# Values by groups of heads, map sums on GpSimd, an earlier first block of rows and 125 VectorE steps in a gated mix of two attentions

## The chip, the cores and the metric

One core of one Trainium2 chip runs the kernel. The metric is the device time of one execution in microseconds, as the median of several runs. The profile is of one further execution.

## The reference, cut to what matters

The input x has 2048 rows of 512 channels; there are 32 heads of 16 channels. Two attentions are computed from x and mixed row by row.

```
g = sigmoid((x * gate_w).sum(-1))
A: q, k, v = x @ A_wqkv, by heads;  pq = q @ w_phi[h];  pk = k @ w_phi[h]
   phi = concat(softmax(p), softmax(-p))          # 32 values per head and row
   kv = phi_k^T v;  z = sum of phi_k over rows
   o = (phi_q kv) / (phi_q z + 1e-6);  a = o @ A_wo
B: q, k, v = x @ B_wqkv, by heads
   o = softmax(q k^T / 4) v;  b = o @ B_wo
out = g * a + (1 - g) * b
```

The softmax of B over 2048 x 2048 scores for each of 32 heads is nearly all of the work: 134 million exponentials.

## The kernel before, in words

**Sets and steps.** B is computed in 32 sets: four blocks of 512 query rows (`qc`), in each four groups of 8 heads (`g`), in each the even and the odd heads (`par`). A set has 16 steps, one for each tile of 128 keys. A step makes the scores of 4 heads in two halves of 128 keys x 1024 (two heads with 512 queries each) on TensorE (L752, `qk`), takes the exponential of both halves, and multiplies with the values on TensorE into one PSUM bank `O` of the set (L794 and L807, `pv`).

**Two ways to take an exponential.** Most steps use ScalarE: two ACTIVATE instructions of 128 x 1024 (L771). NDVE gives for each set the number of steps that VectorE takes instead: two conversions of scores to 16-bit integers (L761, `di`), then over both halves a mask (L777, `dm`), a product (L780, `dw`) and a second mask (L784, `de`). Such a step has two value products. NDVE sums to 117, and its first two entries are 1 and 1. In a set the VectorE steps take the first key tiles, and ScalarE the others in order.

**Values and keys.** `k_proj` (L488) projects 512 rows of keys for one group of heads; its evacuation is on ScalarE for group 0 (L494) and on VectorE for the others (L497). `v_proj` (L525) makes the values of all 32 heads for two tiles of 128 rows at once: 8 matmuls of 512 columns and one VectorE evacuation of 128 x 1024 (L532, seen at the helper's line L469). All sixteen tiles are made in sets 1 and 2. Queries come from `q_proj` (L500). For the first set they are evacuated and multiplied with four masks from SBUF (L510); for the others eight small transfers on SyncE's queue spread the heads (L521).

**Attention A** runs in the gaps. `phi` (L625), 16 times for the keys and 16 times for the queries, makes a map of 128 rows: four matmuls, two exponentials of 128 x 512 on ScalarE (L634), a sum over 16 columns of each of 64 groups on VectorE (L636, TENSOR_REDUCE), an addition on GpSimd for the final check (L638), a reciprocal on VectorE (L640) and a product on GpSimd (L641). Four exponent buffers lie in WAT's memory. Key maps start at unit 100 and follow every 16 units, query maps at 400 and every 32; a set has 32 units, of time as the planner has it.

**The start.** x0 (512 rows, L405) is loaded on SyncE's queue and transposed on TensorE through PSUM (L550), copied by ScalarE and VectorE in halves (L553, L554). Three DMA transposes (L409) bring the other 1536 rows, one after the other, into xT. ScalarE's queue issues five weight loads of B (L412 to L416): group 0 of keys and queries, all values, the other keys, the other queries. Then SyncE issues the DMA transpose of A's weights (WAT, L417), A's values, and the gate.

**Order.** All instructions are given to a planner (`_Sched`) with a priority and a cost. It simulates the five engines and fixes the order on each engine; at run time each engine is strictly in order and waits on semaphores. GpSimd's instructions and VectorE's `dm`, `dw`, `de` and `qm` are `shared`: in the plan the one waits for the other. `est` delays TensorE's use of VectorE's and GpSimd's results by SLACK (0.6). PSUM: a ring `R` of three score tiles used by ScalarE's and VectorE's steps alike, one bank `O`, one bank `M` for all else. Eight buffers `E` hold exponentials; the first 24 exponentials go to memory of phiK and vA instead.

Of the kernel before, what the change touches and what calls it, by code (L numbers as in the profile page):

```python
# [6 lines left out]
BF16 = mybir.dt.bfloat16  # L7
# [6 lines left out]
D = 512  # L14
H = 32
# [18 lines left out]
VROW = H * VW + 16  # L34
NDVE = [1, 1, 4, 4, 4, 3, 4, 4, 3, 4, 3, 4, 4, 3, 5, 4, 4, 3, 4, 3, 5, 3, 4, 4, 5, 3, 4, 4, 4, 3, 5, 4]
LEAD = 3.0
# [10 lines left out]
STAY = 1.0  # L47
PAIRS = (0, 1, 2, 3, 4, 5, 6, 7)
RUSH = 1.5
HOLD = 0.4  # L50
WARM = 10
RUSH_K = 20.0
RUSH_O = 25.0
RUSH_1 = 8.0
QLEAD1 = 28
LATE_A = 0
VLEAD = 3.0
KLEAD1 = 24
KLEAD = 40
QLEAD = 32  # L60
EARLY = 8.0
T0 = 12.0
# [267 lines left out]
def _build(ctx, nc, A_x, A_wqkv, A_w_phi, A_wo, B_wqkv, B_wo, gate_w, out):  # L330
# [19 lines left out]
    vB_ = sb([128, NT, VROW], name="vB")  # L350
    vB = vB_[:, :, 0:H * VW].rearrange("p t (h c) -> p t h c", c=VW)
    vA = sb([128, NT, 8, 66], name="vA")
# [22 lines left out]
    eA_r = _Slots([watv[:, 1024 * i:1024 * (i + 1)] for i in range(4)])  # L375
# [28 lines left out]
    xs = D_all[0].bitcast(BF16).rearrange("p (i c) -> p i c", c=D)  # L404
    op_x0 = dma("sp", -100, 3.6, xs, A_x[0, 0:NQ, :].rearrange("(i p) c -> p i c", p=128), name="x0")  # L405
    op_x = [None]
    for c in range(1, QC):
        op_x.append([add("sp", -100 + c, 2.5,
                         lambda e, c=c: e.dma_start_transpose(xT[:, :, NQ * c:NQ * (c + 1)], A_x[0, NQ * c:NQ * (c + 1), :]),  # L409
                         name=f"x{c}", dma=7.0)])  # L410
    wbv = B_wqkv.rearrange("(t p) c -> p t c", p=128)
    op_wk0 = dma("act", -100, 4.0, W_Bk[:, :, 0:128], wbv[:, :, D:D + 128], name="wk0")  # L412
    op_wq0 = dma("act", -99, 4.0, W_Bq[:, :, 0:128], wbv[:, :, 0:128], name="wq0")
    op_wv = dma("act", -98, 6.0, W_Bv[:], wbv[:, :, 2 * D:3 * D], name="wv")
    op_wk1 = dma("act", -97, 8.0, W_Bk[:, :, 128:D], wbv[:, :, D + 128:2 * D], name="wk")
    op_wq1 = dma("act", -96, 8.0, W_Bq[:, :, 128:D], wbv[:, :, 128:D], name="wq")  # L416
    op_wat = add("sp", -90, 3.0, lambda e: e.dma_start_transpose(WAT[:], A_wqkv[:, 0:2 * D]), name="wat", dma=3.0)  # L417
# [7 lines left out]

    t0, t1, t2, t3 = (mtmp[:, i, :] for i in range(4))
# [13 lines left out]
    op_vpad = [pool(-99, 0.2, lambda e: e.memset(vB_[:, :, H * VW:VROW], 0.0), name="vpad")]  # L440
# [30 lines left out]
    def fill(prio, tile, off, lhs, rhs, deps, name, rush=0.0):  # L471

        f = None
        for t in range(KT):
            f = add("pe", prio - rush + 0.01 * t, MM, lambda e, t=t: e.matmul(  # L475
                tile.ap[:, off:off + 512], lhsT=lhs(t), rhs=rhs(t), start=(t == 0), stop=(t == KT - 1)),
                deps=list(deps) + [f], tiles=[tile], mode="full", name=name, nb=max(0.0, prio - EARLY))
            fills.append(f)
        return f
# [8 lines left out]
    def k_proj(g, c, prio, tile, off, eng="dve"):  # L488
        f = fill(prio, tile, off, lambda t: W_Bk[:, t, 128 * g:128 * (g + 1)],
                 lambda t: xT[:, t, NQ * c:NQ * (c + 1)], op_x[c] + [op_wk1 if g else op_wk0], f"kf{g}{c}", RUSH_K if g != 1 else RUSH_1)  # L490
        use_wk.append(f)
        dst, src = (lambda: kT[:, g, NQ * c:NQ * (c + 1)]), (lambda: tile.ap[:, off:off + 512])
        if eng == "act":
            ev_k[g, c] = add("act", prio, 0.478, lambda e: e.activation(dst(), src(), ACTF.Copy, scale=KFAC),  # L494
                             deps=[f], tiles=[tile], name=f"kev{g}{c}")
        else:
            ev_k[g, c] = add("dve", prio - RUSH_K, 0.6, lambda e: e.tensor_single_scalar(dst(), src(), KFAC, ALU.mult),  # L497
                             deps=[f], tiles=[tile], name=f"kev{g}{c}")

    def q_proj(g, c, prio, tile, off):  # L500

        f = fill(prio, tile, off, lambda t: W_Bq[:, t, 128 * g:128 * (g + 1)],
                 lambda t: xT[:, t, NQ * c:NQ * (c + 1)], op_x[c] + [op_wq1 if g else op_wq0], f"qf{g}{c}", RUSH_K if (g, c) != (1, 0) else RUSH_1)
        qt = q_t[g, c] = _Tile(q_r)
        if (g, c) == (0, 0):
            q3 = lambda: qt.ap[:, 3, :]
            ev = evac("dve", prio, q3, lambda: tile.ap[:, off:off + 512], [f], [tile, qt], name=f"qev{g}{c}")
            ms = []
            for j in range(4):
                ms.append(add("dve", prio + 0.01 * j, 0.39, lambda e, j=j: e.tensor_scalar(  # L510
                    qt.ap[:, j, :], q3(), masks[:, j:j + 1], None, op0=ALU.mult),
                    deps=[ev, op_masks] + (ms if j == 3 else []), tiles=[qt], name=f"qm{g}{c}{j}"))
            ev_q[g, c] = ms
            for o in op_qz:
                o.deps.extend(ms)
            return
# [8 lines left out]
    def v_proj(st, n, prio):  # L525

        tile = _Tile(M_r if n == 1 else R_r)
        fs = [fill(prio, tile, 512 * i, lambda t, i=i: xT[:, t, 128 * (st + i):128 * (st + i + 1)], lambda t: W_Bv[:, t, :],
                   op_x[st // 4] + [op_wv], f"vf{st}") for i in range(n)]
        use_wv.extend(fs)  # L530
        src = lambda: tile.ap[:, 0:512 * n].rearrange("p (t h d) -> p t h d", t=n, d=16)
        e1 = evac("dve", prio, lambda: vB[:, st:st + n, :, 0:16], src, fs, [tile], n=512 * n, name=f"vev{st}")  # L532
        for i in range(n):
            ev_v[st + i] = e1
# [7 lines left out]
    tx = _Tile(R_r)  # L542
    txv = lambda: tx.ap.bitcast(BF16).rearrange("p (t q) -> p t q", q=NQ)
    xtp = []
    for t in range(KT):

        def fn(e, t=t):
            ins = None
            for i in range(4):
                ins = e.transpose(txv()[:, t, 128 * i:128 * (i + 1)], xs[:, i, 128 * t:128 * (t + 1)], ident[:])  # L550
            return ins
        xtp.append(add("pe", -80 + t, 0.3, fn, deps=[op_x0, op_id], tiles=[tx], mode="full", name="xtp"))
    op_x[0] = [add("act", -80, 0.9, lambda e: e.copy(xT[:, 0:2, 0:NQ], txv()[:, 0:2, :]), deps=xtp[0:2], tiles=[tx], name="xev"),  # L553
               add("dve", -80, 0.6, lambda e: e.tensor_copy(xT[:, 2:4, 0:NQ], txv()[:, 2:4, :]), deps=xtp[2:4], tiles=[tx], name="xev")]  # L554
    I_r.tenant[0] = _Tile(None)
    I_r.tenant[0].ops = xtp
    tq = _Tile(R_r)
    k_proj(0, 0, -50, tq, 0, "act")
    q_proj(0, 0, -49, tq, 512)
    tk1 = _Tile(R_r)  # L560
    k_proj(0, 1, -48, tk1, 0, "act")
    k_proj(0, 2, -47, tk1, 512, "act")
    tk2 = _Tile(M_r)
    k_proj(0, 3, -46, tk2, 0, "act")
    for st in range(0, NT, 2):
        if st // 2 in PAIRS:
            v_proj(st, 2, ut(2 * st) - VLEAD)
        else:
            v_proj(st, 1, ut(2 * st) + 0.5)
            v_proj(st + 1, 1, ut(2 * st + 2) + 0.5)  # L570
# [529 lines left out]
```

## Time and profile before

| | |
|---|---|
| median of 3 runs | 791.6 us (791.0 to 792.72) |
| profiled execution | 790.62 us |
| its span, first to last instruction | 788.8 us |
| granted clock of TensorE, mean | 0.998 |
| HBM read, written | 3.69 MB, 2.10 MB |

The span is what the instructions of the trace cover; the time of the execution contains a little more at both ends. In the profile PE is TensorE's matmuls, PEld its weight loads, DVE VectorE, ACT ScalarE, POOL GpSimd and SP SyncE; a q behind a name is the engine's sequencer. L752 is line 752. A row of a group gives its output tile, input tiles, shapes, count, busy time and mean duration, and then the idle time of the engine before it and who ended that. "Busy" is the time with at least one instruction in flight, so that durations in a row can add up to more. A slice is a fortieth of the span, about 20 us.

### The profile page before, as it was taken

Reading aid. Unit: us, or ns where it says so; the run is one execution under the profiler, and the core shown is the slowest. Engines: PE = TensorE matmul, PEld = TensorE weight load, DVE = VectorE, ACT = ScalarE, POOL = GpSimd, SP = SyncE. Lnnn points to the kernel's source line nnn. Section 1 sums busy time; section 2 is a strip of 40 time slices with the busy share of each in tenths; the row PEclk is TensorE's granted clock in tenths of the full one; section 3 lists DMA queues with packets and bytes.
Section 4 is the critical chain, followed back from the end, with each engine's and each line's share of the span. In section 5 each row is a group of like instructions: output and inputs, shape, how many; then the busy total and the mean of one; then the engine's idle time right before and its main releaser. Section 6 shows DMA issues by size and latency. Waiting matters only on the chain.

```text
span 788.8 us, 13621 instructions
## 1 busy us (share of the span) xinstructions
PE 708.3 (90%) x5645; PEld 224.7 (28%) x5716; DVE 710.5 (90%) x883; ACT 764.3 (97%) x865; POOL 121.1 (15%) x123
## 2 busy tenths in 40 slices
PE   8899999999999898998888999899998999988886
PEld 3223232222222222332222323222232232222222
DVE  2456999999999999999999999999999999999993
ACT  4989999999999999999999999999999999999995
POOL 7000002022233322111112010310111101120000
PEclk9999999999999999999999999999999999999999
DMA  9100000000000000023110121210111101120000
GB/s 240 28 8 2 11 4 1 10 6 1 14 1 8 9 1 14 1 68 41 28 21 21 30 19 34 48 23 19 27 22 40 35 14 27 35 42 1 7 1 30
DMA packets 55923, 19.57 MB, mean 25 GB/s; under 512 B 48304, under 2 KB 55856, under 8 KB 55856
## 3 DMA queue, kind: packets, MB, share of 16 engines
q1 hardware_dynamic: 52960, 17.06, 10.4%
q10 hardware_dynamic: 2640, 1.57, 0.7%
q8 instruction: 46, 0.75, 0.4%
q14 instruction: 21, 0.17, 0.1%
q0 software_dynamic: 256, 0.02, 0.0%
HBM read 3.69 MB, written 2.10 MB: 7 GB/s over the span
## 4 chain that ended last, share of the span: by engine, by line
ACT 87%; PE 6%; DVE 4%; DMA 2%; SPq 1%; issue 0%
ACT E L771 80%; ACT WAT L634 4%; PE ps L752 2%; ACT phiK L771 2%; PE ps L475 1%; DVE D L761 1%; DMA xT<-in_A_x_dram 1%; ACT vA L771 1%; PE ps L891 1%; PE ps L807 1%; SPq L521 1%; DVE D L777 1%; DVE D L780 1%; SPq L409 1%; PE ps L665 0%; DMA WB<-WB 0%
## 5 line engine op out<-in xcount | busy, mean ns | idle before, releaser
L771 ACT ACTIVATE E<-ps 128x1024 bf16<-128x1024 f32 x766 | 713.2, 1185 | 4.3 <-PE ps L807 2.2
L752 PE MATMUL ps<-q,kT 64*128 64x512 bf16 x2048 | 362.8, 385 | 58.1 <-ACT E L771 45.7
L761 DVE TENSOR_SCALAR D<-ps 128x1024 int16<-128x1024 f32 x234 | 284.5, 1216 | 21.7 <-PE ps L752 21.1
L752 PEld LDWEIGHTS ps<-q,kT 64*128 64x128 bf16 x2048 | 89.8, 93 | 275.2 <-ACT E L771 214.3
L807 PE MATMUL ps<-E,vB 128*32 128x512 bf16 x1532 | 149.1, 389 | 5.0 <-issue 4.3
L780 DVE TENSOR_TENSOR D<-D 128x2048 bf16<-128x2048 bf16 x117 | 141.4, 1209 | 0.6
L794 PE MATMUL ps<-D,vB 128*32 128x512 bf16 x936 | 90.8, 386 | 1.6 <-issue 1.0
L638 POOL TENSOR_TENSOR acc<-acc,ss 128x64 f32<-128x64 f32 x32 | 24.9, 778 | 435.4 <-DVE ss L636 435.4
L777 DVE TENSOR_SCALAR D<-D 128x2048 int16<-128x2048 int16 x117 | 83.8, 717 | 1.1
L784 DVE TENSOR_SCALAR D<-D 128x2048 int16<-128x2048 int16 x117 | 81.7, 698 | 0.1
L807 PEld LDWEIGHTS ps<-E,vB 128*32 128x32 bf16 x1532 | 37.8, 93 | 85.4 <-issue 77.5
L475 PE MATMUL ps<-xT,WB 128*128 128x512 bf16 x111 | 40.2, 388 | 3.3 <-ACT WAT L634 1.4
L634 ACT ACTIVATE WAT<-ps 128x512 bf16<-128x512 f32 x64 | 39.6, 755 | 0.0
L636 DVE TENSOR_REDUCE ss<-WAT 128x64 f32<-128x1024 bf16 x32 | 38.8, 1212 | 0.6 <-ACT WAT L634 0.4
L475 PE MATMUL ps<-Wp,xT 128*128 128x512 bf16 x98 | 38.0, 389 | 0.5 <-DVE OT L469 0.3
L641 POOL TENSOR_TENSOR phiK<-WAT,ss 128x1024 bf16<-128x1024 bf16 x16 | 35.6, 2222 | 10.7 <-DVE ss L640 10.7
L641 POOL TENSOR_TENSOR WB<-WAT,ss 128x1024 bf16<-128x1024 bf16 x16 | 33.5, 2096 | 14.3 <-DVE ss L640 14.3
L794 PEld LDWEIGHTS ps<-D,vB 128*32 128x32 bf16 x936 | 23.7, 94 | 37.5 <-issue 29.0
L469 DVE CAST vB<-ps 128x1024 bf16<-128x1024 f32 x8 | 9.8, 1225 | 22.0 <-PE ps L475 22.0
L835 PE MATMUL ps<-ident,OT 128*128 128x128 f32 x128 | 27.6, 300 | 0.5 <-ACT WAT L634 0.3
L891 PE MATMUL ps<-phiK 128*128 128x512 bf16 x74 | 25.8, 386 | 0.8 <-issue 0.3
L848 POOL TENSOR_TENSOR acc<-acc,rB 128x64 f32<-128x64 f32 x8 | 5.1, 633 | 133.9 <-DVE rB L840 133.9
(98 smaller groups left out, 351.2 us busy)
## 6 DMA issues: line engine op xcount, KB each, us to landing
out_dram<-Wp SPq DMA_DIRECT2D x16, 128.0 KB, 1.7
q<-qs SPq DMA_DIRECT2D x120, 16.0 KB, 1.8
WB<-in_B_wqkv_dram ACTq DMA_DIRECT2D x2, 384.0 KB, 8.6
D<-in_A_x_dram SPq DMA_DIRECT2D x1, 512.0 KB, 4.5
WB<-in_B_wqkv_dram ACTq DMA_DIRECT2D x1, 512.0 KB, 6.8
WAv<-in_A_wqkv_dram SPq DMA_DIRECT2D x1, 512.0 KB, 4.1
phiK<-in_A_wo_dram SPq DMA_DIRECT2D x1, 512.0 KB, 4.0
phiK<-in_B_wo_dram SPq DMA_DIRECT2D x1, 512.0 KB, 4.8
```

The costliest lines, as they stand in the source:

```text
L475: f = add("pe", prio - rush + 0.01 * t, MM, lambda e, t=t: e.matmul(tile.ap[:, off:off + 512], lhsT=lhs(t), rhs=rhs(t), start=(t == 0), st ...
L634: o5 = [add("act", prio + 1, 0.478, lambda e, a=a: e.activation(ev()[:, :, a, :], P(), ACTF.Exp, scale=1.0 - 2.0 * a), deps=[f], tiles=[ti ...
L636: o6 = add("dve", prio + 5, 1.13, lambda e: e.tensor_reduce(ss.ap[:, 0, :], ee.ap.rearrange("p (g f) -> p g f", f=DH), AX.X, ALU.add), dep ...
L641: return add("pool", prio + 7, 1.95, lambda e: e.tensor_tensor(dst().rearrange("p (g f) -> p g f", f=DH), ee.ap.rearrange("p (g f) -> p g ...
L752: ins = e.matmul(r.ap[:, 512 * i:512 * (i + 1)], lhsT=kT[p0:p0 + 64, g, 128 * kt:128 * (kt + 1)], rhs=qt.ap[p0:p0 + 64, 2 * pair + par, :] ...
L761: last_di = [add("dve", when - 6, 1.133, lambda e, r=r, I=I, part=part: e.tensor_scalar(I.ap[:, 1024 * part:1024 * (part + 1)], r.ap, EXP_ ...
L771: exps.append(add("act", when, 0.904, lambda e, r=r, E=E: e.activation(E.ap, r.ap, ACTF.Exp, scale=EXP_SCALE), deps=[q], tiles=[r, E], nam ...
L777: d1 = add("dve", pd, 0.06 + 0.54 * nk, lambda e, I=I, F=F, n=n: e.tensor_scalar(F.ap[:, 0:n], I.ap[:, 0:n], 0x007F, 0x3F00, op0=ALU.bitwi ...
L780: d4 = [add("dve", pd + 0.01 * y, 1.133, lambda e, I=I, F=F, lo=2048 * y: e.tensor_tensor(F.ap[:, lo:lo + 2048].bitcast(BF16), I.ap[:, lo: ...
L784: d2 = add("dve", pd + 0.1, 0.06 + 0.54 * nk, lambda e, I=I, n=n: e.tensor_scalar(I.ap[:, 0:n], I.ap[:, 0:n], -128, 0x0001, op0=ALU.bitwis ...
L794: ins = e.matmul(O.ap[32 * s:32 * s + 32, :], lhsT=vB_[:, kt, VW * h:VW * h + 32], rhs=w.ap.bitcast(BF16)[:, base + 1024 * (s % 2) + 512 * ...
L807: ins = e.matmul(O.ap[32 * s:32 * s + 32, :], lhsT=vB_[:, kt, VW * h:VW * h + 32], rhs=es[s % 2].ap[:, 512 * (s // 2):512 * (s // 2 + 1)], ...
```

## The change

The number of VectorE steps rises to 125, with 3 and 4 in the first two sets. Each step of a set takes the key tile of its place in time, whichever engine has it. The values are projected by groups of 8 heads and 512 rows (16 matmuls of 128 columns, one evacuation of 128 x 512): group 0 in set 1, each other group ahead of its first set; `vB` is laid out in groups with the last group first. The sum of a map is four additions on GpSimd that halve the columns. The first 512 rows are loaded in two halves on two queues, each followed by the small weight block of group 0; the second 512 rows are loaded plainly and transposed on TensorE (`turn(1)`); the first key projection is cut into 128 and 384 rows; the query masks are applied from PSUM, without the copy. The remaining weights of B move from ScalarE's queue to SyncE's, behind the DMA transposes. ScalarE loads its table by a small exponential of its own ahead of the first copies. Exponent buffers of the maps go from four to two, beside one buffer for partial sums. Key maps start at unit 170 and follow every 20, query maps at 470 and every 30. Constants of the planner change as shown; the switches KM, SM, SW, SE and PH2 stand at values that leave the structure as it was.

```
-NDVE = [1, 1, 4, 4, 4, 3, 4, 4, 3, 4, 3, 4, 4, 3, 5, 4, 4, 3, 4, 3, 5, 3, 4, 4, 5, 3, 4, 4, 4, 3, 5, 4]
-LEAD = 3.0
+NDVE = [3, 4, 3, 5, 3, 3, 4, 4, 4, 4, 4, 3, 5, 4, 3, 5, 4, 4, 4, 4, 4, 3, 4, 5, 5, 3, 4, 4, 5, 3, 5, 3]
+PH = [0.0, -2.7, 0.0, 0.0, -1.9, 0.0, 1.2, 0.0, 0.0, -0.7, -2.2, -0.7, -2.9, -0.8, 0.3, -1.5, 0.0, -2.3, 1.5, -1.6, 0.0, -3.0, 0.0, -0.1, 0.0, -5.2, 2.1, -0.8, 0.8, 3.8, 2.2, -1.5]
+LEAD = 4.0
...
-STAY = 1.0
-RUSH = 1.5
-HOLD = 0.4
-WARM = 10
+STAY = 2.6
+RUSH = 2.5
+HOLD = 0.3
+WARM = 7
...
-T0 = 12.0
+T0 = 9.0
...
-    eA_r = _Slots([watv[:, 1024 * i:1024 * (i + 1)] for i in range(4)])
+    eA_r = _Slots([watv[:, 1024 * i:1024 * (i + 1)] for i in range(2)])
+    tr_r = _Slots([watv[:, 2048:3840].bitcast(F32).rearrange("p (a b) -> p a b", b=64)])
...
+    op_xs = [[dma("sp", -110, 3.0, xs[0][:, 0:2, :], x_rows(0, 256), name="x0"), dma("act", -110, 3.0, xs[0][:, 2:4, :], x_rows(256, 512), name="x0")]]
+    op_wq0 = dma("sp", -109, 3.4, W_Bq[:, :, 0:128], wbv[:, :, 0:128], name="wq0")
+    op_wk0 = dma("act", -109, 3.4, W_Bk[:, :, 0:128], wbv[:, :, D:D + 128], name="wk0")
+    op_xs.append([dma("sp", -108, 4.0, xs[1], x_rows(512, 1024), name="x1")])
+    op_wv0 = dma("act", -108, 4.5, W_Bv[:, :, 0:128], wbv[:, :, 2 * D:2 * D + 128], name="wv0")
...
+    add("act", -107, 1.3, lambda e: e.activation(junk[:], ones32[:], ACTF.Exp), deps=[op_one], name="table")
...
-            ev = evac("dve", prio, q3, lambda: tile.ap[:, off:off + 512], [f], [tile, qt], name=f"qev{g}{c}")
...
+            for n, j in enumerate((0, 2, 1, 3)):
+                ms[j] = add("dve", prio + 0.01 * n, 0.62, lambda e, j=j: e.tensor_scalar(
+                    qt.ap[:, j, :], src(), masks[:, j:j + 1], None, op0=ALU.mult), deps=[f, op_masks], tiles=[tile, qt], name=f"q0{j}")
...
+    def v_proj(g, c, prio):
...
+        for i in range(4):
+            def fn(e, i=i):
+                ins = None
+                for t in range(KT):
+                    ins = e.matmul(tile.ap[:, 128 * i:128 * (i + 1)], lhsT=xT[:, t, 128 * (4 * c + i):128 * (4 * c + i + 1)],
+                                   rhs=W_Bv[:, t, 128 * g:128 * (g + 1)], start=(t == 0), stop=(t == KT - 1))
+                return ins
...
+    turn(0)
     tq = _Tile(R_r)
+    q_proj(0, 0, -50, tq, 512)
+    k_proj(0, 0, -49, tq, 0, "act", 0, 128)
+    k_proj(0, 0, -48.9, _Tile(M_r), 0, K0, 128, NQ)
+    turn(1)
...
-        o6 = add("dve", prio + 5, 1.13, lambda e: e.tensor_reduce(
-            ss.ap[:, 0, :], ee.ap.rearrange("p (g f) -> p g f", f=DH), AX.X, ALU.add), deps=o5, tiles=[ee, ss])
+        for n, d in ((8, 1.12), (4, 0.71), (2, 0.5), (1, 0.4)):
+            o6 = add("pool", prio + 5, d, lambda e, n=n: e.tensor_tensor(
+                tr(n), tr(2 * n)[:, :, 0:n], tr(2 * n)[:, :, n:2 * n], ALU.add), deps=[o6] if o6 else o5, tiles=[ee, ss, tr_], name="ared")
...
-        prio = ut(100 + 16 * st)
+        prio = ut(PK0 + PKS * st)
...
-        prio = ut(400 + 32 * st)
+        prio = ut(PQ0 + PQS * st)
...
-                for at, kts, vec in sorted(steps):
+                for k, (at, _, vec) in enumerate(sorted(steps)):
+                    kts = (k,)
```

More of the change, by code (lines that the diff above doesn't have):

```diff
@@ L412, in _build @@
[L412 to L417, printed above, removed]
+    xs = [D_all[c].bitcast(BF16).rearrange("p (i c) -> p i c", c=D) for c in range(2)]
@@ L504, in q_proj @@
         qt = q_t[g, c] = _Tile(q_r)
         if (g, c) == (0, 0):
-            q3 = lambda: qt.ap[:, 3, :]
-            ev = evac("dve", prio, q3, lambda: tile.ap[:, off:off + 512], [f], [tile, qt], name=f"qev{g}{c}")
[L508 to L512, printed above, removed]
+            src = lambda: tile.ap[:, off:off + NQ]
@@ L541, in _build @@
             deps=[z0], tiles=[tw, tz], mode="full", name="warm")
[L542 to L556, printed above, removed]
-    tq = _Tile(R_r)
[L558 to L562, printed above, removed]
@@ L716, in _build @@
     early = [_Tile(_Slots([phiK[:, st, :]])) for st in range(NT)]
-    hosts = list(zip(op_phk, early))
+    hosts = [(o, early[i // PH2]) for i, o in enumerate(op_phk)]
     vAf = vA[:].rearrange("p t g c -> p (t g c)")
```

220 lines of the change are left out of this document (141 added, 79 removed).

## The prediction

> **What bounds the kernel now.** I read the page first: busy shares, the slices and the chain that ended last.
>
> ```profile
> span 788.8 us, 13621 instructions
> PE 708.3 (90%) x5645; PEld 224.7 (28%) x5716; DVE 710.5 (90%) x883; ACT 764.3 (97%) x865; POOL 121.1 (15%) x123
> ...
> DVE  2456999999999999999999999999999999999993
> ACT  4989999999999999999999999999999999999995
> ...
> ACT 87%; PE 6%; DVE 4%; DMA 2%; SPq 1%; issue 0%
> ```
>
> ScalarE is busy 97% of the span and holds 87% of the chain. VectorE is nearly as full, except in the first four slices. Four windows separate the stages: up to the first exponential, sets 1 and 2, sets 3 to 32 (from the 61st exponential on), and what follows the last exponential.
>
> ```profile
> core 0: us, PE busy (x) PEld busy (x) DVE busy (x) ACT busy (x) POOL busy (x), PEclk, DMA share, GB/s
> 0.00:11.55 11.55, 9.17 (x46) 3.89 (x47) 3.24 (x8) 2.89 (x3) 8.08 (x23) 1.00 0.91 243
> 11.55:73.80 62.25, 56.80 (x397) 17.82 (x402) 29.30 (x33) 57.03 (x64) 7.54 (x11) 1.00 0.20 42
> 73.80:777.37 703.57, 636.60 (x5175) 200.49 (x5235) 674.89 (x836) 702.03 (x796) 104.47 (x86) 1.00 0.09 19
> 777.37:788.80 11.43, 5.71 (x43) 2.51 (x36) 3.04 (x8) 2.34 (x5) 1.01 (x3) 0.88 0.17 52
> ```
>
> In the long third stage ScalarE idles only 703.57 - 702.03 = 1.5 us, so time there is ScalarE's work and nothing else. VectorE is 674.89 / 703.57 = 95.9% busy: second, and close. In sets 1 and 2 ScalarE idles 62.25 - 57.03 = 5.2 us while VectorE is used less than half (29.30 of 62.25). Before that, 11.55 us pass until the first exponential. So there are three places to gain: fewer exponentials, an earlier first one, fewer gaps in the first 74 us. One condition stands over them: VectorE must not become the bound.
>
> Prices come from the groups by shape and from stretches of the chain in which one engine runs back to back; there the step from start to start is what an operation really costs.
>
> ```profile
> L771 ACT ACTIVATE E<-ps 128x1024 bf16<-128x1024 f32 x766 | 713.2, 1185 | 4.3 <-PE ps L807 2.2 <-PE ps L752 2.0
> L761 DVE TENSOR_SCALAR D<-ps 128x1024 int16<-128x1024 f32 x234 | 284.5, 1216 | 21.7 <-PE ps L752 21.1
> L636 DVE TENSOR_REDUCE ss<-WAT 128x64 f32<-128x1024 bf16 x32 | 38.8, 1212 | 0.6 <-ACT WAT L634 0.4
> L777 DVE TENSOR_SCALAR D<-D 128x2048 int16<-128x2048 int16 x117 | 83.8, 717 | 1.1
> L469 DVE CAST vA<-ps 128x512 bf16<-128x512 f32 x16 | 10.6, 665 | 0.1
> L469 DVE CAST vB<-ps 128x1024 bf16<-128x1024 f32 x8 | 9.8, 1225 | 22.0 <-PE ps L475 22.0
> L771 ACT ACTIVATE phiK<-ps 128x1024 bf16<-128x1024 f32 x16 | 15.2, 1079 | 4.4 <-PE ps L752 4.4
> L771 ACT ACTIVATE vA<-ps 128x1024 bf16<-128x1024 f32 x8 | 7.6, 1197 | 0.0
> ```
> ```profile
> 133.07 26.58 ACT E L771 x29
> ...
> 374.59 0.60 DVE D L784
> 375.19 0.60 DVE D L777
> 375.79 1.13 DVE D L761
> 376.93 1.13 DVE D L780
> ...
> 381.38 1.13 DVE ss L636
> ```
>
> The first block gives 766 + 16 + 8 = 790 exponentials, which is 2 x (512 - 117), and 234 conversions on VectorE, which is 2 x 117. The chain gives 26.58 / 29 = 0.917 us for one exponential on ScalarE (the mean of 1185 ns overlaps its neighbour), and for one VectorE step 2 x 1.13 + 1.13 + 0.60 + 0.60 = 4.59 us. A sum over a map (L636) costs VectorE 1.13 us.
>
> **The change part by part.** *Steps.* The list NDVE sums to 117 before and 125 after: 8 steps, 16 exponentials, leave ScalarE: 16 x 0.917 = **14.7 us** less. Sets 1 and 2 go from 2 steps to 7, sets 3 to 32 from 115 to 118. On VectorE the 8 steps cost 8 x 4.59 = 36.7 us, and TensorE gets 8 more value products, beside work that has room.
>
> *Sums to GpSimd.* VectorE loses 32 x 1.13 = 36.2 us, so the steps are paid almost exactly. The trace has no GpSimd sum of these sizes. I draw a line through its products (1.93 us at 1024 columns, the median of one group) and its 64-column addition (0.32 us, the shortest):
>
> ```profile
> L641 POOL TENSOR_TENSOR WB<-WAT,ss x16: 1927/1931/2781, 353.5 to 694.0; 128x1024 bf16<-128x1024 bf16 x16
> L638 POOL TENSOR_TENSOR acc<-acc,ss x32: 318/698/1329, 126.0 to 691.2; 128x64 f32<-128x64 f32 x32
> L777 DVE TENSOR_SCALAR D<-D x117: 629/685/2416, 27.8 to 770.2; 128x2048 int16<-128x2048 int16 x117
> ```
>
> That is 1.68 ns a column and 0.21 us fixed: 1.07 + 0.64 + 0.43 + 0.32 = 2.5 us for the four adds of a map, 79 us in all, on an engine that is busy for 121 of 789. GpSimd has room; the delay is the matter. VectorE's reciprocal (L640) now waits for the fourth add, where before its own engine made the sum. Behind it in VectorE's order stand the next conversions, which hold a PSUM ring of three that ScalarE shares; TensorE, also in order, would then stop at a value product and ScalarE would run dry. The planner places the reciprocal after the adds by its own costs (1.12, 0.71, 0.50, 0.40 us, 2.73 together, above my 2.5), so I expect it late by little. The smaller rings (two exponent buffers for four, one for the partial sums) only forbid that maps overlap; maps follow every 20 or 30 units of a set's 32, which is over 14 us, and one lasts about 7.
>
> There is also contention. VectorE and GpSimd disturb each other:
>
> ```profile
> 385.75 2.25 POOL L641 TENSOR_TENSOR WB<-WAT,ss 128x1024 bf16<-128x1024 bf16 x1 [2.84 <-DVE ss L640]
> ```
> ```profile
> 386.13 2.42 DVE L777 TENSOR_SCALAR D<-D 128x2048 int16<-128x2048 int16 x1
> ```
>
> This mask operation ended when GpSimd's product had, 2.42 us for a median of 0.685. But such meetings are rare: L777's busy time over 117 (717 ns each, in the groups above) is 0.03 us above the median, 3.7 us in all, beside 104 us of GpSimd work. Another 79 us would add some 3 us to VectorE by proportion. The bounds are 0 (all kept apart) and 79 us (VectorE stands for every add). I take 3, nearest to the row, since the planner keeps mask operations and GpSimd apart (`shared`) for the new adds too.
> [...] If every add blocked VectorE, the sum would be that of the third rival below.
>
> *VectorE's account.* Sets 3 to 32: 674.9 + 3 x 4.59 - 36.2 + 8 x 0.6 (value evacuations that move here, 0.665 us each standing alone) + 3 = 660 us. ScalarE's time there falls by 2 x 3 x 0.917 = 5.5 us to 698, so VectorE would be 94.6% busy, below the 95.9% it bears now: some 9 us of room. Sets 1 and 2: 29.3 + 5 x 4.59 - 8 x 1.23 + 8 x 0.67 + 1.4 (two evacuations of the second block of rows) = 49 us, where ScalarE needs (60 - 10) x 0.917 and some 3 us, about 50. This is tight: VectorE starts full and may fall behind until set 3, whose steps drop from 4 to 3.
>
> *The start.* The rows of the first exponential:
>
> ```profile
> 5.40 1.05 PE L550 MATMUL ps<-ident,D 128*128 128x128 bf16 x16
> ...
> 6.49 0.69 DVE L554 COPY xT<-ps 128x1024 bf16<-128x1024 bf16 x1 [3.76 <-PE ps L550]
> ...
> 7.24 1.90 PE L475 MATMUL ps<-xT,WB 128*128 128x512 bf16 x8 [0.79 <-DVE xT L554]
> ...
> 9.18 0.69 DVE L469 CAST q<-ps 128x512 bf16<-128x512 f32 x1 [1.99 <-PE ps L475]
> 9.90 0.88 DVE L510 TENSOR_SCALAR q<-q,masks 128x512 bf16<-128x512 bf16 x3
> ...
> 11.12 0.39 PE L752 MATMUL ps<-q,kT 64*128 64x512 bf16 x2
> ...
> 11.55 1.02 ACT L771 ACTIVATE phiK<-ps 128x1024 bf16<-128x1024 f32 x1 [1.99 <-PE ps L752]
> ...
> 16.33 1.02 ACT L771 ACTIVATE phiK<-ps 128x1024 bf16<-128x1024 f32 x1 [1.83 <-PE ps L752]
> ```
> ```profile
> D<-in_A_x_dram SPq DMA_DIRECT2D x1, 512.0 KB, 4.5
> phiK<-in_A_wo_dram SPq DMA_DIRECT2D x1, 512.0 KB, 4.0
> out_dram<-Wp SPq DMA_DIRECT2D x16, 128.0 KB, 1.7
> ```
>
> The first 512 rows land 4.5 us after their issue. After the change two queues bring half each, with small weight blocks behind them; a half must take between 1.7 us (128 KB alone) and 4.5. I take 4.0, that of a 512 KB load in quiet, which is 0.5 us earlier. Then 1.05 us of transposes; copies in quarters end 0.45 after them (a half takes 0.69 now); only the query's last matmul is left, 0.4 (it follows the quarters; the eight of now take 1.90 behind both halves), with the 128-key projection and its small evacuation beside the mask; the mask straight from PSUM, 0.69; scores, 0.43 to the exponential. From 4.9: 4.9 + 1.05 + 0.45 + 0.4 + 0.69 + 0.43 + some 0.5 for handing over = **8.4**, 3.1 us before 11.55.
> [...]
>
> The second block of rows comes plain and is turned by TensorE; the third's DMA transpose is issued where the second's was, so keys 8 to 15 come one place earlier. The row at 16.33 shows ScalarE waiting 1.83 us in set 1. With values by groups, TensorE makes in sets 1 and 2 half the value columns; 64 matmuls of 512 columns, a start every 0.22 us or so (1.90 us for the eight at 7.24), are 14 us, and become 7, so the waits of set 2 also shrink. I halve the 5.2 us of idle time to 2.5: **2.7 us** gained, bounds 0 and 5.2. One more key evacuation costs 0.3 us. The remaining weights and WAT queue on SyncE behind the transposes, land some ten microseconds later, and are used from some 30 us on: covered. The early table load costs nothing and gives nothing, being done before the transposes even now. The other constants (STAY, RUSH, HOLD, PH, leads) reorder TensorE; I take 0, between -1.5 (all idle time of sets 3 to 32) and +6.
>
> *Sum.* 14.7 + 3.1 + 2.7 - 0.3 = 20.2 us. The profiled execution took 790.62 us for a span of 788.8: 790.6 - 20.2 = 770.4. The median of the runs shown is 791.6, 1.0 above it: **771.4**.
>
> **The rivals.**
> *VectorE is the bound at the start.* If it keeps 49 us of work only 90% full and starts at 10 rather than 8.4, sets 1 and 2 end at 64 instead of 59: 776.5. If GpSimd's sums cost another 0.5 us a map beyond the room (16 us less 9), 778 to 783. For: 95.9% now, and the tight account; against: set 3 can absorb some.
> *The first rows gain nothing.* Queues share engines, and the first exponential stays near 11.5: 774.5. This is also how the change would fail to do what it says.
> *The sums stand in VectorE's way (slower).* 32 maps, 2.5 us each: if VectorE stops for the adds, at its reciprocal or behind a blocked mask operation, for s us a map, the time is 771.4 + 32 s - 9. From s = 0.9 on the gain is gone; at s = 1.5, 810. For: L638 goes from 0.318 to 1.33 us beside VectorE, and the 2.42 us row; against: the low mean excess, and that the room of 9 us must go first.
>
> **How the numbers follow.** Forecast 0.62 (767 to 775); VectorE bound early or in part, 0.18 (775 to 783); no gain at the start, 0.08 (774.5); the slower rival 0.07 (from 793 up); 0.05 lies between 783 and 793, 0.02 of it within 0.2% of 791.6 (0.2% is about what a measurement can tell from no change). Range 765 to 782: the lower end has no idle time after the first exponential and 1 to 2 us from the order, the upper takes most of the first rival. Faster 0.91, same 0.02, slower 0.07.
>
> **What would show it.** 774 exponentials at 0.917 us; the first at 8 to 9 us; the 51st (set 3) at about 59 where the 61st now is at 73.8; VectorE busy some 712 us; L640's wait for GpSimd summing to under 10 us; ScalarE's idle time in sets 3 to 32 under 3 us. The prediction is wrong if ScalarE shows idle time behind VectorE or GpSimd in the long stage, or if the first exponential doesn't move.

## The result and the profile after

The changed kernel takes 787.88 us (median of 5 runs, 786.36 to 788.11) against 791.6 us, a ratio of 0.9945 (95% interval 0.9929 to 0.996). It is faster, by 3.7 us, where 20.2 were forecast, and lies above the range. The profiled execution took 788.11 us. The page of the changed kernel, its busy shares, slices and chain:

```profile
span 786.3 us, 14285 instructions
...
PE 729.3 (93%) x5957; PEld 235.6 (30%) x5957; DVE 730.9 (93%) x901; ACT 753.3 (96%) x852; POOL 226.7 (29%) x251
...
DVE  6888999799999989999999999999999998999992
ACT  6999999999999999999989999998999999999995
...
ACT 65%; DVE 20%; PE 10%; DMA 2%; SPq 2%; issue 1%; DVEq 0%
```

ScalarE's share of the chain fell from 87% to 65%; VectorE's rose from 4% to 20%. ScalarE has 11 us less to do, and yet its slices now show eights, where it waits. The same four windows as before, cut at the first exponential (9.40), at the 51st, with which set 3 begins (59.20), and at the end of the last (775.47):

```profile
core 0: us, PE busy (x) PEld busy (x) DVE busy (x) ACT busy (x) POOL busy (x), PEclk, DMA share, GB/s
0.00:9.40 9.40, 7.11 (x47) 3.32 (x47) 3.38 (x7) 3.24 (x7) 8.01 (x23) 1.00 0.90 200
9.40:59.20 49.80, 47.73 (x438) 18.75 (x436) 45.49 (x53) 47.94 (x54) 8.98 (x11) 1.00 0.34 72
59.20:775.47 716.27, 668.98 (x5445) 211.26 (x5443) 678.94 (x835) 699.80 (x790) 208.72 (x214) 0.99 0.09 19
775.47:786.30 10.83, 5.47 (x32) 2.30 (x31) 3.04 (x8) 2.33 (x4) 1.00 (x3) 0.99 0.16 53
```

The start did what was forecast: set 3 begins at 59.2 us, 14.6 us before the 73.8 of the old kernel. The long stage gave 12.7 us back: 716.27 us against 703.57, with six exponentials fewer. ScalarE idles 716.27 - 699.80 = 16.5 us there; it was 1.5. So the question is what keeps ScalarE waiting in sets 3 to 32.

One place shows it, in the changed kernel's timeline (start, duration, engine, line, operation; in brackets the idle time before it and what ended that): first GpSimd, then VectorE, TensorE and ScalarE.

```profile
534.27 2.78 POOL L701 TENSOR_TENSOR WB<-WAT,ss 128x1024 bf16<-128x1024 bf16 x1 [1.58 <-DVE ss L697]
537.01 4.07 POOL L693 TENSOR_TENSOR WAT<-WAT 128x512 f32<-128x512 bf16 x3
```
```profile
534.11 1.16 DVE L848 TENSOR_TENSOR D<-D 128x2048 bf16<-128x2048 bf16 x1
535.19 2.41 DVE L845 TENSOR_SCALAR D<-D 128x2048 int16<-128x2048 int16 x1
537.52 1.64 DVE L851 TENSOR_SCALAR D<-D 128x2048 int16<-128x2048 int16 x1
539.08 1.75 DVE L848 TENSOR_TENSOR D<-D 128x2048 bf16<-128x2048 bf16 x1
540.75 1.21 DVE L823 TENSOR_SCALAR D<-ps 128x1024 int16<-128x1024 f32 x1
```
```profile
542.02 0.39 PE L814 MATMUL ps<-q,kT 64*128 64x512 bf16 x2 [2.70 <-DVE D L823]
```
```profile
543.42 1.02 ACT L833 ACTIVATE E<-ps 128x1024 bf16<-128x1024 f32 x1 [2.71 <-PE ps L814]
```

A mask (L845) begins while GpSimd's product runs and ends 0.55 us after it, 2.41 us for a median of 0.685. (The old kernel's mask of 2.42 us, which the prediction shows, also ended 0.55 us after GpSimd's product, and not with it.) GpSimd's product takes 2.78 us in place of 1.93, but not because of this mask: VectorE's product (L848) was running when it began. At 251.85 us another one takes 2.78 us behind L848, and no mask follows it. So at both meetings the one that began second ended late, the mask by 1.73 us and the product by 0.85. The next mask and VectorE's product meet the additions that follow. Three instructions lose some 3 us, the conversion (L823) that frees a score buffer comes late by as much, TensorE stands for 2.70 us, and ScalarE for 2.71.

Then the damage grows. TensorE's granted clock (the figure 0.51 behind ACT and POOL) in the 3.4 us after that stop:

```profile
543.80:547.20 3.40, 3.40 (x14) 0.56 (x12) 2.92 (x4) 2.59 (x3) 0.00 (x0) 0.51 0.07 18
```

It is half, and ScalarE gets its scores late twice more, by 0.50 and 0.46 us. The clock falls three times inside the long stage, at 393.6, 543.7 and 649.6 us, to 0.51 for 3.4 us each time, behind stops of 1.15, 2.70 and 2.46 us that end at 392.2, 542.0 and 647.7; in the profiled execution of the kernel before, never. Masks were held up shortly before the first two; at the third TensorE waits for a transfer.

### The profile page after: what moved, and what is told of

Read it like the earlier page. It is cut to its first block, busy times and chain, and to the rows that moved or that the text cites. A ratio compares the mean times of both kernels' runs of the same rounds, so it can differ in the third digit from the quotient of the medians.

```text
span 786.3 us, 14285 instructions
## 1 busy us (share of the span) xinstructions
PE 729.3 (93%) x5957; PEld 235.6 (30%) x5957; DVE 730.9 (93%) x901; ACT 753.3 (96%) x852; POOL 226.7 (29%) x251
## 4 chain that ended last, share of the span: by engine, by line
ACT 65%; DVE 20%; PE 10%; DMA 2%; SPq 2%; issue 1%; DVEq 0%
ACT E L833 60%; DVE D L823 7%; PE ps L814 4%; DVE D L848 4%; DVE D L845 3%; ACT WAT L687 3%; DVE D L851 2%; SPq L554 2%; ACT phiK L833 1%; PE ps L874 1%; PE ps L506 1%; DMA WB<-WB 1%; PE ps L958 1%; DMA D<-in_A_x_dram 1%; PE ps L861 1%
## 5 line engine op out<-in xcount | busy, mean ns | idle before, releaser
L833 ACT ACTIVATE E<-ps 128x1024 bf16<-128x1024 f32 x750 | 699.6, 1134 | 16.8 <-PE ps L814 15.6
L823 DVE TENSOR_SCALAR D<-ps 128x1024 int16<-128x1024 f32 x250 | 303.4, 1213 | 28.7 <-PE ps L814 25.3
L693 POOL TENSOR_TENSOR WAT<-WAT 128x512 f32<-128x512 bf16 (+2 forms) x96 | 96.5, 1006 | 259.6 <-ACT WAT L687 254.8
L848 DVE TENSOR_TENSOR D<-D 128x2048 bf16<-128x2048 bf16 x125 | 152.8, 1225 | 0.4
L845 DVE TENSOR_SCALAR D<-D 128x2048 int16<-128x2048 int16 x125 | 100.8, 811 | 0.9
L861 PE MATMUL ps<-D,vB 128*32 128x512 bf16 x1000 | 96.9, 388 | 1.4 <-DVE D L851 1.1
L851 DVE TENSOR_SCALAR D<-D 128x2048 int16<-128x2048 int16 x125 | 90.0, 721 | 0.1
L506 PE MATMUL ps<-Wp,xT 128*128 128x512 bf16 x128 | 49.7, 396 | 2.0 <-DVE kz L734 1.2
L701 POOL TENSOR_TENSOR WB<-WAT,ss 128x1024 bf16<-128x1024 bf16 x16 | 38.6, 2414 | 44.7 <-DVE ss L697 44.7
L506 PE MATMUL ps<-xT,WB 128*128 128x512 bf16 x132 | 47.4, 382 | 1.2 <-ACT WAT L687 0.6
L506 PE MATMUL ps<-WAv,xT 128*128 128x512 bf16 x64 | 23.5, 388 | 1.2 <-ACT WAT L687 1.1
L506 PEld LDWEIGHTS ps<-Wp,xT 128*128 128x128 bf16 x128 | 11.8, 96 | 35.1 <-issue 28.7
```

The costliest lines, as they stand in the source:

```text
L506: f = add("pe", prio - rush + 0.01 * t, MM * n / 512, lambda e, t=t: e.matmul(tile.ap[:, off:off + n], lhsT=lhs(t), rhs=rhs(t), start=(t = ...
L693: o6 = add("pool", prio + 5, d, lambda e, n=n: e.tensor_tensor(tr(n), tr(2 * n)[:, :, 0:n], tr(2 * n)[:, :, n:2 * n], ALU.add), deps=[o6] ...
L701: halves.append(add("pool", prio + 7 + 0.1 * h, 0.15 + 1.8 / PH2, lambda e, gs_=gs_: e.tensor_tensor(dst().rearrange("p (g f) -> p g f", f ...
L823: last_di = [add("dve", when - 6, 1.133, lambda e, r=r, I=I, part=part: e.tensor_scalar(I.ap[:, 1024 * part:1024 * (part + 1)], r.ap, EXP_ ...
L833: exps.append(add("act", when, 0.904, lambda e, r=r, E=E: e.activation(E.ap, r.ap, ACTF.Exp, scale=EXP_SCALE), deps=[q], tiles=[r, E], nam ...
L845: d1 = [add("dve", pd + 0.01 * y, 0.06 + 0.54 / SM, lambda e, I=I, F=F, lo=lo, hi=hi: e.tensor_scalar(F.ap[:, lo:hi], I.ap[:, lo:hi], 0x00 ...
```

## Experiments

Three theories. **A**: GpSimd holds up VectorE's masks, as above. **B**: the new order by itself leaves ScalarE dry on the chip. **C**, formed later: the transfers of attention A's maps land late. Where an edit is called "same order", every engine executes in the order of the changed kernel.

| kernel | median us | ratio to the kernel before (95%) | ScalarE idle in the long stage, us | masks beyond their medians, us |
|---|---|---|---|---|
| before | 791.6 | 1 | 1.5 | 5.5 |
| changed | 787.88 | 0.9945 (0.9929 to 0.996) | 16.5 | 20.8 |
| small_adds | 785.34 | 0.9927 (0.9901 to 0.9952) | 14.3 | 14.7 |
| small_products | 779.24 | 0.9845 (0.9828 to 0.9861) | 6.6 | 7.5 |
| no_hold | 777.14 | 0.9815 (0.979 to 0.984) | 7.5 | 3.9 |
| exclude | 786.02 | 0.9932 (0.9909 to 0.9954) | 6.6 | 0 |
| exclude_late | 779.19 | 0.984 (0.9827 to 0.9854) | 8.2 | 0.8 |
| pool_waits | 777.18 | 0.9823 (0.9808 to 0.9838) | 7.6 | 7.2 |
| dve_waits | 789.39 | 0.9976 (0.9967 to 0.9985) | 17.5 | 18.8 |
| no_map_wait | 772.57 | 0.9755 (0.9738 to 0.9771) | 3.0 | 7.0 |
| later_maps | 776.48 | 0.9802 (0.9786 to 0.9819) | 4.6 | 7.4 |
| quarters | 785.59 | 0.9919 (0.9893 to 0.9945) | 13.9 | 21.7 |
| slack_1 | 797.05 | 1.0068 (1.0044 to 1.0092) | 24.2 | 27.8 |
| sums_dve_122 | 791.07 | 0.9996 (0.998 to 1.0012) | 14.7 | 4.5 |
| two_buffers | 791.23 | 0.9999 (0.9985 to 1.0013) | 1.8 | 5.4 |
| adds_beside | 797.29 | 1.0093 (1.0069 to 1.0118) | 6.4 | 7.0 |
| adds_beside_excl | 796.74 | 1.0063 (1.0041 to 1.0085) | 6.7 | 0 |
| before_waits | 791.36 | 0.9998 (0.9983 to 1.0013) | 0.8 | 5.0 |

The last column sums, over both masks of all VectorE steps, what they take beyond the median of their line; idle time and masks are of the profiled execution.

**small_adds, small_products, no_hold: less GpSimd work, same order.** Most of each sum, or of each map, is left out.

```
-                tr(n), tr(2 * n)[:, :, 0:n], tr(2 * n)[:, :, n:2 * n], ALU.add)
+                tr(1), tr(16)[:, :, 0:1], tr(16)[:, :, 8:9], ALU.add)           # small_adds, no_hold
-                dst()...[:, gs_, :], ee...[:, gs_, :], ss.ap[:, 1, gs_].unsqueeze(2).to_broadcast(...), ALU.mult)
+                dst()...[:, gs_, 0:1], ee...[:, gs_, 0:1], ss.ap[:, 1, gs_].unsqueeze(2), ALU.mult)   # small_products, no_hold
```

> The changed kernel with the same order on every engine, in which each of the four additions of a map takes 64 columns only (the sums are of two columns of sixteen, so part of the sum is left out). GpSimd's sums fall from 110 us to about 45. Theory A (GpSimd's instructions hold up VectorE's mask operations beside them; VectorE gets late against its order, TensorE stops at a score for a buffer that VectorE holds, ScalarE runs dry): ScalarE's idle time in sets 3 to 32 falls from 16.5 us to under 11 and the time from 788 to 776 to 783; the products of the maps still hold up VectorE. Theory B (the new order alone, by constants, keys in time order and values by groups, leaves ScalarE dry): the order is the same, so 786 to 789.

> The changed kernel, same order, with the products of the maps cut to 64 columns (all but one column in sixteen of the maps is left out) and the four additions whole: no_hold less small_adds. If the additions and the products each do their own harm, the 2.5 us of small_adds and this gain add up to the 10.7 of no_hold: about 780. If it is the sum of both on GpSimd that makes it late: 783 to 786. If the products alone do it: 777 to 778.

> small_adds with the products of the maps cut to 64 columns too (the sums and all but one column in sixteen of the maps are left out); the order on every engine is still that of the changed kernel. GpSimd's work in sets 3 to 32 falls from 209 us to under 90. Theory A (VectorE held up beside GpSimd): the masks lose nearly all of their 20 us of excess, no clock dips, ScalarE's idle time in sets 3 to 32 under 8 us, 772 to 777. Theory B (gaps of the order itself on the chip): 782 to 786, as small_adds.

Without either, the time falls by 10.7 us to 777.1, just above what theory A had (772 to 777), and the idle time to 7.5 us (under 8, as expected). One detail missed: the clock still falls twice in the long stage. Smaller additions alone give 2.5 us, less than theory A expected (776 to 783, idle time under 11), and the two intervals overlap; smaller products alone give 8.6. The two add up to 11.1, about the 10.7 of both. So most of the harm is done by the products, which the old kernel had as well, and less by the additions; the masks' excess says the same. The profiled execution of small_products is the fastest of its four, 776.8 us: its clock does not fall in the long stage, though TensorE stops for 2.29 us in one place. The other three have a mean granted clock of 0.993 to 0.995 and take 779.2 to 779.8. So some of these times depends on how often the clock falls in an execution of the same kernel.

**exclude, exclude_late, pool_waits, dve_waits: nothing left out, turns enforced.** After the plan is made, a `shared` instruction gets a wait on the last one of the other engine that the plan puts ahead of it; in the last three only behind 60 us of the plan, and in the last two on one engine alone. The lines are those of pool_waits.

```
+        last = {"dve": None, "pool": None}
+        for o in sorted((o for o in self.ops if o.shared and o.start > 60), key=lambda o: (o.start, o.seq)):
+            other = last["pool" if o.eng == "dve" else "dve"]
+            if o.eng == "pool" and other is not None and other not in o.deps:
+                o.deps.append(other)
+            last[o.eng] = o
```

> The changed kernel, same order, with semaphores that hold GpSimd's instructions and VectorE's masks and products to the turns that they have in the plan, so that they never run side by side. Theory A, if what hurts is that they meet at other places than planned: the excess of the masks goes and 774 to 781 comes out; if GpSimd comes late anyway the hold-up turns into a wait of VectorE and the time stays at 785 to 792. Theory B: 788 or more, waits being added for nothing.

> exclude, with the turns kept only for what is planned after 60 us, so that the start is that of the changed kernel. Theory A: set 3 begins at 59 to 60 us, the long stage takes 704 to 706 us as in exclude, 775 to 779 in all. Theory B: what exclude gained in the long stage was luck of its later start; 783 or more.

> As exclude_late, but GpSimd alone waits for its turn; VectorE never waits for GpSimd's. If the harm is that GpSimd starts an instruction early, just ahead of a mask of VectorE that comes late: nearly the whole gain, 776 to 780. If the harm is that GpSimd comes late: as the changed kernel, 785 to 789.

> As exclude_late, but VectorE alone waits for its turn. A mask that waits for GpSimd's instruction and a mask that is held up by it end at the same time, so if GpSimd's early starts are the harm nothing is gained: 784 to 792. If GpSimd's lateness is the harm: 776 to 781.

exclude misses what theory A had for it (774 to 781). Its long stage takes 704.50 us, but sets 1 and 2 take 58.2 in place of 49.8, because VectorE there waits for the small transfers that GpSimd's queue issues:

```profile
24.07 0.69 DVE L857 TENSOR_SCALAR D<-D 128x2048 int16<-128x2048 int16 x1 [5.11 <-DMA Wbd<-in_A_w_phi_dram]
```

With the start left alone, exclude_late comes to 779.2 (775 to 779 expected). The one-sided kernels separate cause and effect. If VectorE alone waits, nothing is gained (789.4): nothing keeps GpSimd from starting ahead of its turn, and the masks still exceed their medians by 18.8 us. If GpSimd alone waits, as much is gained as by leaving its work out (777.2): GpSimd was starting just ahead of masks that VectorE had not reached yet. The masks' two groups in the changed kernel and then in pool_waits (mean ns after the comma), and GpSimd's product in pool_waits:

```profile
L845 DVE TENSOR_SCALAR D<-D 128x2048 int16<-128x2048 int16 x125 | 100.8, 811 | 0.9
L851 DVE TENSOR_SCALAR D<-D 128x2048 int16<-128x2048 int16 x125 | 90.0, 721 | 0.1
```
```profile
L851 DVE TENSOR_SCALAR D<-D 128x2048 int16<-128x2048 int16 x125 | 87.1, 701 | 0.9
L857 DVE TENSOR_SCALAR D<-D 128x2048 int16<-128x2048 int16 x125 | 90.3, 724 | 0.1
...
L707 POOL TENSOR_TENSOR WB<-WAT,ss 128x1024 bf16<-128x1024 bf16 x16 | 30.8, 1928 | 37.6 <-DVE D L854 20.8 <-DVE D L857 12.0 <-DVE ss L703 4.0
```

GpSimd's product is back at 1.93 us in all its places (2414 ns in the changed kernel's mean), and its wait costs nothing that the time shows. The first mask lost its excess: 811 to 701 ns, 13.8 us over 125. The second kept it.

**before_waits, two_buffers, adds_beside, adds_beside_excl: the same tried on the kernel before.** before_waits is the edit above on the old kernel. two_buffers gives its maps two exponent buffers; adds_beside has in addition the four additions, unused, on GpSimd; adds_beside_excl enforces the turns in it on both engines.

```
+        x6 = None
+        for n, d in ((8, 1.12), (4, 0.71), (2, 0.5), (1, 0.4)):
+            x6 = add("pool", prio + 5, d, lambda e, n=n: e.tensor_tensor(
+                tr(n), tr(2 * n)[:, :, 0:n], tr(2 * n)[:, :, n:2 * n], ALU.add), deps=[x6] if x6 else o5, tiles=[ee, tr_], name="ared")
```

> The kernel before with GpSimd waiting for its turn as in pool_waits. In the long stage ScalarE idles only 1.5 us there, so if the gain of pool_waits belongs to the added GpSimd work, nothing is to be had here: 789 to 792. If GpSimd's turns help whatever the kernel, 780 to 785.

> The kernel before with two exponent buffers for the maps in place of four and nothing else: the control of adds_beside. Both theories: 790 to 795, since a map takes some 7 us and the next comes over 11 us later.

> The kernel before, with the four additions of each map made on GpSimd as well, into memory that nobody reads, VectorE's sum kept; two exponent buffers. Nobody waits for them but the release of a buffer. Theory A: VectorE's two masks get 10 to 15 us longer in all, and VectorE, 96% busy there already, makes the time 5 to 15 us more than that of two_buffers. Theory B: contention is no matter, within 2 us of two_buffers.

> adds_beside (the kernel before with unused additions on GpSimd, 797) with the turns kept after 60 us. Theory A: the 5.5 us that the additions cost go, 790 to 793. Otherwise, if they cost by the exponent buffers that they keep or by the order planned around them: 795 to 799.

The old kernel gains nothing by the waits, though it has the same products: there the masks exceed their medians by only 5.5 us, and 5.0 with the waits, and ScalarE idles only 1.5 us. Added work on GpSimd makes it 6.1 us slower than two_buffers, a time that theory A had forecast; but the masks' excess is 7.0 us against 5.4, where 10 to 15 more was expected. Enforced turns take even that away (the longest mask falls from 2.42 to 0.70 us) and leave the time at 796.7. So this loss is not the hold-up; the order planned around the additions costs it, or the clock, which falls twice in the long stage of adds_beside_excl; which of the two is open. As a measure of theory A, adds_beside fails.

**quarters, slack_1, sums_dve_122: other orders.**

```
-PH2 = 1
+PH2 = 4                       # quarters
-SLACK = 0.6
+SLACK = 1.0                   # slack_1
-        for n, d in ((8, 1.12), (4, 0.71), (2, 0.5), (1, 0.4)):
...
+        o6 = add("dve", prio + 5, 1.13, lambda e: e.tensor_reduce(...   # sums_dve_122; NDVE: 3, 4, then as before
```

> The changed kernel with each product of a map in four instructions on GpSimd (256 columns each) in place of one, the order planned anew for it. Theory A: a mask is held up by 0.6 us at most in place of 1.7, the longest mask falls from 2.4 to about 1.3 us, 781 to 785. Theory B: 785 to 792, by whatever the new order gives.

> The changed kernel with SLACK 1.0 in place of 0.6: TensorE's orders expect what comes from VectorE and GpSimd 0.4 us later. Theory A: TensorE bears more of VectorE's lateness, fewer gaps of ScalarE, 782 to 787. Theory B (an order that is good only by its own clock): any other order is as good on the chip, 786 to 790.

> The changed kernel with the sums of the maps back on VectorE (four exponent buffers) and the steps of sets 3 to 32 as before (115), sets 1 and 2 at 3 and 4: 122 steps. Theory A: the start of the changed kernel (set 3 at 59 us) and the long stage of the kernel before (704 us, a little more for the values of two groups): 775 to 781. Theory B: the order's gaps stay, 785 to 792.

Quarters gives 2.3 us, within overlapping intervals and in theory B's range; the longest mask is 1.92 us and not 1.3 (that this comes from quarters that follow one another is my estimate, which no run shows), and the masks lose as much in all as in the changed kernel. slack_1 is slower than either theory allowed: 24.2 us idle, the clock halved over five stretches in the stage; its masks are held up by more (27.8 us), so what the order alone costs is not told by it. sums_dve_122 came out as theory B had it (785 to 792) and not as A (775 to 781): it has few hold-ups and still 14.7 us of idle time, 5.9 of it in sets 3 to 8 and 7.4 in sets 25 to 32. So an order planned anew can lose as much as the hold-ups. For the question whether the sums had to move these kernels decide nothing, because the constants and PH were set for other counts.

**no_map_wait, later_maps: the rest.** With the hold-ups gone there remain 777.2 - 771.4 = 5.8 us. TensorE's rows of pool_waits show the longest stops that are left, for the transfer of a map to be transposed (WB<-WB), and the clock after one:

```profile
635.91 0.36 PE L757 MATMUL ps<-kz,WB 128*128 128x4 bf16 x8 [2.23 <-DMA WB<-WB]
```
```profile
PE ps L757 <- DMA WB<-WB: 4.8, 3, 2.2
```
```profile
636.20:639.60 3.40, 3.40 (x29) 1.01 (x26) 3.19 (x5) 1.60 (x2) 0.31 (x1) 0.55 0.00 0
```

no_map_wait is pool_waits with TensorE's two small products reading keys in place of the transposed map, and without their wait; later_maps is pool_waits planned anew with a longer transfer.

```
-                ins = e.matmul(dn.ap[...], lhsT=ptt.ap[:, g, :], rhs=kz[:, g, 64:68], ...)      # likewise for num
+                ins = e.matmul(dn.ap[...], lhsT=kT[:, 0, 128 * g:128 * (g + 1)], rhs=kz[:, g, 64:68], ...)
+            if o.name in ("den", "num"):
+                o.deps = [d for d in o.deps if d.name != "phT"]
...
-                 deps=op_ph + use_wk, tiles=[ph, ptt], dma=3.5, name="phT")
+                 deps=op_ph + use_wk, tiles=[ph, ptt], dma=4.0, name="phT")                      # later_maps alone
```

> pool_waits in the same order, in which TensorE's small products of attention A's query side read keys that lie ready in place of the transposed map, and so do not wait for its transfer (the query maps are left out of the result). Theory C (what remains above the forecast comes from maps that land late: TensorE stops for 4.8 us in three places, its clock halves behind them, ScalarE idles): the waits and the clock drops at 540 and 636 us go, 771 to 775. Theory B (gaps of the order): 776 to 778, as pool_waits.

> pool_waits planned anew with 4.0 us in place of 3.5 for the transfer of a map, nothing left out. Theory C: TensorE's waits for the transfer fall from 4.8 to under 2 us; the order itself is another one, so 774 to 780.

Theory C holds: without the waits 772.6, in the same order, and the clock drops at 540 and 636 us are gone. A third, at 724.6 us of pool_waits, where TensorE stands nowhere near for as much as 1 us, has its like in no_map_wait at 719.5. The long stage of pool_waits and then of no_map_wait:

```profile
59.10:764.70 705.60, 667.20 (x5445) 211.06 (x5443) 665.14 (x835) 697.99 (x790) 161.25 (x214) 0.99 0.09 19
```
```profile
59.60:759.90 700.30, 664.98 (x5445) 210.61 (x5444) 664.95 (x835) 697.29 (x790) 161.28 (x214) 1.00 0.09 19
```

The idle time falls from 7.6 to 3.0 us. later_maps does it with nothing left out: waits of 1.1 us in place of 4.8 and no clock drop in the stage, but an order of its own, and 776.5 us. It and pool_waits are the fastest with nothing left out; their intervals overlap.

## Why the prediction was wrong, point by point

**Right: the steps and the start.** The exponentials are 750 + 16 + 8 = 774. Set 3 begins at 59.2 us (59 forecast). The first exponential came at 9.40 and not 8.4: the halves landed 3.4 and 3.9 us after their issue, near the 4.0 taken, but two steps behind them took longer. The query's mask began 1.28 us after the copies (0.4 forecast), since the key projections take turns with the query's on TensorE; and the first scores waited for transposes of the second block, which stand ahead of them on TensorE, some 0.6 us. Sets 1 and 2 made up for it: ScalarE idles 49.80 - 47.94 = 1.9 us (2.5 forecast) and VectorE carries 45.5 us of work (49). The rival of a VectorE bound at the start didn't come. Nor did the one without a gain there, though the queues do share engines: in the kernel before, ScalarE's queue (q10) has 85.2% of the 16 engines' time from 8 to 10 us and SyncE's (q1) 70.1% from 10 to 12. The changed kernel's timeline at that point, the copies, the projections and the masks, eight transposes of the second block, then the first scores and the first exponential:

```profile
5.37 0.87 DVE L600 COPY xT<-ps 128x512 bf16<-128x512 bf16 x2 [2.62 <-PE ps L595]
5.79 1.91 PE L506 MATMUL ps<-xT,WB 128*128 128x512 bf16 x12
7.52 2.72 DVE L544 TENSOR_SCALAR q<-ps,masks 128x512 bf16<-128x512 f32 x4 [1.27 <-PE ps L506]
8.39 0.62 PE L595 MATMUL ps<-ident,D 128*128 128x128 bf16 x8 [0.70 <-DMA D<-in_A_x_dram]
8.95 0.61 PE L814 MATMUL ps<-q,kT 64*128 64x512 bf16 x4
9.38 1.02 ACT L833 ACTIVATE phiK<-ps 128x1024 bf16<-128x1024 f32 x1 [1.15 <-PE ps L814]
```

**The step that failed: "Another 79 us would add some 3 us to VectorE by proportion."** The masks' durations in the changed kernel (shortest, median, longest, in ns), and the old kernel's second mask:

```profile
L845 DVE TENSOR_SCALAR D<-D x125: 626/685/2417, 14.4 to 766.4; 128x2048 int16<-128x2048 int16 x125
L851 DVE TENSOR_SCALAR D<-D x125: 621/681/1641, 19.0 to 768.4; 128x2048 int16<-128x2048 int16 x125
```
```profile
L784 DVE TENSOR_SCALAR D<-D x117: 623/683/1285, 29.8 to 772.2; 128x2048 int16<-128x2048 int16 x117
L784 DVE TENSOR_SCALAR D<-D 128x2048 int16<-128x2048 int16 x117 | 81.7, 698 | 0.1
```

The masks exceed their medians by (811 - 685) x 125 + (721 - 681) x 125 = 20.8 us, where the old kernel has 5.5 (the prediction's 3.7 is its first mask alone). That is 15.3 more and not 3, and the proportion was the wrong law: the same products cost at most the 1.5 us that ScalarE idles in the old kernel's long stage, and 8.6 us in the changed one, by small_products. VectorE was busy 730.9 us in all, where 712 were expected. What counts is where GpSimd's and VectorE's instructions meet. I argued that the planner keeps them apart. It does so on paper only; no semaphore holds the turns, and nothing in the old trace showed how far the engines may drift from them. The price of the additions was right where nothing meets them (2.58 us a map in exclude_late, 2.5 forecast); in the changed kernel they take 3.43 us.

**And VectorE's room was no cover.** The sum let 9 us of room absorb such delays. VectorE still idles 716.27 - 678.94 = 37 us in the long stage, but some 3 us lost at once at 535 us stopped TensorE, which is in order, for 2.70 us, and its clock stood at 0.51 in the 3.4 us from 543.80. Room on the average pays for no single late conversion. The whole of this is 10.7 us of the 16.5 that were missed, by pool_waits (787.9 to 777.2); how much of it is the hold-ups and how much the clock behind them, the runs do not separate.

**The order's term of 0 was too small.** I expected a late sum to be felt at VectorE's reciprocal. The reciprocal waits for nothing; the changed kernel's view of line L697, in which nothing stands under its idle time (the list of those who waited for it goes on):

```profile
L697 DVE RECIPROCAL ss<-ss x32: 487/539/546, 184.5 to 729.6; 128x64 f32<-128x64 f32 x32
its engine sat idle before it (us, times) until:
who waited for it (us, times):
  POOL WB L701: 44.7, 16
  POOL phiK L701: 31.1, 14
```

TensorE waits two steps further on, for the map's transfer: 4.3 us in three places in the changed kernel (0.8 in the old), 4.6 us of time by no_map_wait (777.2 to 772.6). But no late sum is behind that: in no_hold, with additions and products cut, TensorE still waits 5.1 us in three places. What is late is the issue of the transfer. At the stop that ends at 635.91 us of pool_waits, GpSimd had ended that map's product at 629.27; SyncE's queue issued the transfer at 632.66, behind another transpose:

```profile
630.40 2.21 SPq L775 DMA_TRANSPOSE phiK<-WAv  x1
632.66 1.31 SPq L751 DMA_TRANSPOSE WB<-WB  x1
```

In the other two places the issue comes 4.9 and 5.8 us after the product's end, and every time the transfer lands 3.1 to 3.3 us after its issue. The planner has 0.6 us for each of these two issues; that its costs for SyncE's queue make the transfer late is not tested. So this loss belongs to the planned order, for which I took 0, between -1.5 and +6: the size was wrong, inside its bounds. What is left after both, 772.6 against 771.4, is within what the runs can tell.

**The slower rival** had the mechanism nearly right (it named the additions, where the products did most of the harm) and too high a price. Solved for s, its formula 771.4 + 32 s - 9 gives 0.8 us a map for the 787.9 measured, just short of the 0.9 at which the gain is gone. I had given it 7%, and nothing between 783 and 793 more than 5%; a hold-up of that size without a loss was the case that I left thin.

## What to carry to other kernels

A plan that keeps two engines apart by time alone keeps them apart on paper; look for a semaphore, and if there is none, count on collisions wherever the two drift: here the masks exceed their medians by 20.8 us. Put the wait on the engine that has room: here waits on GpSimd gave 10.7 us, and the same waits on VectorE gave nothing. When an engine chain is in order, price a late instruction by what stands behind it, and not by the average room of the engine that it is late on: here some 3 us on VectorE, which had 37 us of room, cost ScalarE 2.71 us at once.

## What the runs showed of the hardware that was not expected

A GpSimd instruction and a 16-bit mask of 128 x 2048 or a product on VectorE can lengthen one another. All 28 masks of the changed kernel that take 0.15 us or more beyond the median end 0.55 us after the GpSimd instruction that was running when they began; the longest takes 2.42 us for a median of 0.685, and the longest of VectorE's products 1.75 for 1.21. GpSimd's product takes 1.93 us where neither was running at its start (13 times), 2.25 behind a mask (7 times) and 2.78 behind VectorE's product (12 times). With GpSimd's turns kept, in pool_waits, its two groups of 16 take 1.928 and 1.929 us on the mean. Conversions out of PSUM (L823) are not held up: 1154 to 1226 ns over all 250.

TensorE's granted clock falls to half for 3.4 us at a time behind some stops, and the length of the stop did not decide it: 1.15 us were enough in the changed kernel, 2.29 us in small_products were not, and in pool_waits it fell once with no stop of 1 us near. Behind the one at 543.7 us of the changed kernel, where ScalarE had stood for 2.71 us, it stood twice more, for 0.50 and 0.46.
